# A list scheduler that counts a transfer's landing when it frees a buffer, with re-measured costs

## Chip, cores and metric

One core of a Trainium2 chip (trn2) runs the whole program. The time of a run is the device time in microseconds (us); the figure to predict is the median of the runs of the changed kernel.

## What is computed

Attention with talking heads, then a small mixture of matmuls with a softmax-like gate. Batch 4, 12 heads, 448 positions, head size 64; the second part has 1792 tokens, 768 in and 1024 hidden.

```python
scores = scale * np.matmul(q, k.transpose(0, 1, 3, 2))
scores = np.einsum('bhij,hg->bgij', scores, w_pre)
scores = scores - np.max(scores, axis=-1, keepdims=True)
attn = np.exp(scores)
attn = attn / (np.sum(attn, axis=-1, keepdims=True) + 1e-09)
attn = np.einsum('bhij,hg->bgij', attn, w_post)
x = np.matmul(attn, v)            # to (1792, 768)
h = x @ w_in
e = np.exp(h - np.max(h, axis=-1, keepdims=True))
solu = h * e / (np.sum(e, axis=-1, keepdims=True) + 1e-09)
ln = (solu - mean(solu)) / np.sqrt(var(solu) + 1e-06) * g_ln
out = ln @ w_out
```

## The kernel before

**Attention.** Every fp32 operand is split into a high and a low half in fp16. q, k and v of a batch are loaded in pieces, their largest magnitude is found on DVE (line 373; for v on ACT, line 371), they are scaled, and the halves are written: the high half on ACT (in batch 0) or POOL (line 217 or 219), the low half on DVE (line 222) or POOL (lines 406 and 407). The halves of q and k are turned by DMA transposes on SP's queue (`turn_in`, line 419; for k of batch 0 by PE), and a part of q is moved to other partitions (`move_hi`, line 464, in batch 0 on ACT's queue, else on SP's).

Scores are made in **blocks**, four to a batch, each of 120 or 88 query rows and all 12 heads. For each head `qk` (line 480) makes 448 scores per row in PSUM, `score_hi` (line 486, ACT) copies the high half to the block's tile `s`, and `score_lo` (line 491, DVE) writes the low half. There are two such tiles (ring `S`), so the first `score_hi` of a block needs the tile of the block two before to have been read out. A block is called (batch, number), as (1,0).

Then the work goes by **units** of 10 query rows, 45 to a batch. A `fetch` (line 509, SP) gathers the unit's rows for all 12 heads from `s` into one of three `sr` tiles (from SBUF to SBUF, 210 KB with all heads); `premix` (line 515, PE) mixes the heads; `rowmax` (line 520, DVE), `expo` (line 532, ACT), `guard` and `invert` (lines 546 and 549, DVE) and `weigh` (line 553, POOL) make the exponentials and the scaled mixing weights; `postmix` (line 561, PE) mixes again, and `post_out` (line 226, ACT) copies to `p_t`. When the units of a block are through, `av` (line 601, PE) multiplies by v, in two groups of heads, through one PSUM bank: the second group needs the first one read by `x_hi` (line 217, ACT) and `x_lo` (line 222, DVE). These write the batch's tiles `xsh` and `xsl`, of which there is one set (ring `X`), stored to DRAM by `x_store` (line 643, SP) in the next batch.

During the last batch w_in is loaded and split too, and the first matmuls of the second part (`h0`, line 764) are mixed in.

**What sets the order.** All of this is a list of about 2,850 tasks. Class `Plan` (lines 19 to 96) places them one by one: each has the engines that may run it with an assumed cost in us, the tasks it comes after, a due time, perhaps a ring (a number of buffers) with the tasks that free its buffer (`until`), and a latency `lat` that is added for whoever comes after it. Of the tasks that could start first, the one due first is taken. The instructions are then issued in that order, and each engine and queue of the chip runs its own in order; the plan's times are nowhere in the program. What the plan assumes, therefore, decides only which instruction stands before which.

A dependency counted `end + lat + 0.2`; a buffer's release counted the end of the freeing task plus 0.2, without its `lat`. `T0` and `STEP` (line 131) set the due times: unit u of batch b is due at T0 + STEP (45 b + u).

**The second part** is written out by hand behind the plan (lines 1145 to 1374) and is not touched.

Of the kernel before, what the change touches and what calls it, by code (L numbers as in the profile page):

```python
# [18 lines left out]
class Plan:  # L19
# [15 lines left out]
    def order(self):  # L35
        tasks, done, out = self.tasks, {}, []
# [9 lines left out]
        def ready(k, e):  # L46
            _, _, after, _, ring, _, _, _ = tasks[k]
            r = 0.0
            for a in after:
                end, eng, lat = done[a]  # L50
                r = max(r, end + lat + (0.06 if eng == e else self.WAIT))
            if ring and len(held[ring]) >= self.size[ring]:
                for a in held[ring][-self.size[ring]]:
                    if a not in done:
                        return None
                    r = max(r, done[a][0] + self.WAIT)
            return r

        last = {}
        while len(out) < len(tasks):  # L60
            best = None
            for e, t0 in free.items():
                able = []
                for k in avail:
                    on = tasks[k][1]
                    if e in on:
                        r = ready(k, e)
# [16 lines left out]
            run, on, _, _, ring, until, lat, _ = tasks[k]  # L84
# [15 lines left out]
def kernel(  # L100
# [26 lines left out]
    NU = (S + UN - 1) // UN  # L127
    NE, NWR = 4, 3
    WEIGH = {"pool": 0.36}
    AMV = {"act": 0.83}  # L130
    T0, STEP = 24, 2.17

    RING = 18
    SIZES = [[9, 12, 12, 12] if b % 2 == 0 else [12, 12, 12, 9] for b in range(B)]
# [638 lines left out]
    def add_tasks():  # L773
# [28 lines left out]
        for b in range(B):  # L802
# [3 lines left out]
            for n in "kq":  # L806
# [17 lines left out]
                for i in range(NP):  # L824
                    add(
                        ("am", n, b, i),
                        with_eng(absmax, n, b, i),
                        {"dve": 0.87},
                        after=[("ld", n, b, j) for j in range(pieces) if i * pieces < (j + 1) * NP and j * NP < (i + 1) * pieces]
                        + ["clear"],  # L830
                        due=at(b - 1, 15 + -4 * (n == "q")) + 3 * i if b else 4 * (n == "q") + i,
                    )
# [4 lines left out]
                for p in range(NPAIR):  # L837
                    due = at(b - 1, 24 + -4 * (n == "q") + 1 * p) if b else 12.0 + 6 * (n == "q") + 1.5 * p
                    add(
                        ("hi", n, b, p),  # L840
                        with_eng(pair_hi, n, b, p),
                        {"pool": 0.7} if b else {"act": 0.61},
                        after=ready + ([("hi", n, b, p - 1)] if p else before),
                        due=due,
                        ring=None if p else "hl",
                        until=[("tp", j) for j in range(NPAIR)] if z and n == "k" else [("t", n, b, j) for j, _ in turns[z]],
                    )
                    add(("lo", n, b, p), with_eng(pair_lo, n, b, p), {"dve": 0.66, "pool": 1.75} if b else {"dve": 0.66, "pool": 1.75}, after=[("hi", n, b, p)], due=due + 1)
                if z and n == "k":
                    for p in range(NPAIR):  # L850
                        due = 11 + 1.5 * p
# [10 lines left out]
                for p, m in turns[z] if not (z and n == "k") else ():  # L862
                    due = at(b - 1, 28 + 2 * p) if b else 14 + 3 * (n == "q") + 1.5 * p
                    add(
                        ("t", n, b, p),
                        one(turn_in, n, b, p, m),
                        {"sp": 1.2 if m == 1 else 1.95},
                        after=[("lo", n, b, j) for j in range(p, p + m)]
                        + ([] if z else [("qk", b - 1, NQ - 1, h) for h in range(2 * p, 2 * (p + m), 2)]),
                        due=due,  # L870
                        lat=2.0,
                    )
                    if n == "q":
                        add(
                            ("q1", b, p),
                            one(move_hi, b, p, m),
                            {"act": 0.1 * m} if z else {"sp": 0.7 * m},
                            after=[("t", n, b, p)] + [("cl", g) for g in range(NPAIR // GP)],
                            due=due + 1.5,
                            lat=2.6 if z else 2.1,  # L880
                        )
            add(("es", b), one(exp_scales, b), {"dve": 0.15}, after=es, due=at(b - 1, 35) if b else T0 - -2)

# [60 lines left out]
            for u in range(NU):  # L944
# [5 lines left out]
                add(  # L950
                    ("f",) + g,
                    one(fetch, *g),
                    {"sp": 0.9},
                    after=[("sl", b, blk, h) for h in range(H)],
                    behind=behind("f"),
                    due=d - 2 * STEP,
                    ring="sr",
                    until=[("m",) + g],
                    lat=2.0,
                )  # L960
                add(
                    ("m",) + g,
# [7 lines left out]
                add(  # L970
                    ("mx",) + g,
                    one(rowmax, *g),
                    {"dve": 0.6},
                    after=[("m",) + g, ("es", b)],
                    due=d + 0.5,
                    ring="e",
# [6 lines left out]
                    after=[("mx",) + g],  # L983
                    due=d + 1.2,
                )
                add(("gd",) + g, with_eng(guard, *g), {"dve": 0.08}, after=[("ex",) + g], due=d + 2)
                add(("iv",) + g, one(invert, *g), {"dve": 0.08}, after=[("gd",) + g], due=d + 2.2)
                add(
                    ("w",) + g,
                    with_eng(weigh, *g),  # L990
# [24 lines left out]
            for blk in range(NBLK[b]):  # L1015
# [3 lines left out]
                for g in range(NXG):  # L1019
# [12 lines left out]
                    add(  # L1032
                        ("xh", b, blk, g),
                        one(x_hi, b, blk, g),
                        {"act": 0.18 + 0.0007 * XG * n},
                        after=[("av", b, blk, g)] + ready,
                        due=due,
                        ring="X" if blk == g == 0 else None,
# [2 lines left out]
                    add(  # L1041
                        ("xl", b, blk, g),
                        one(x_lo, b, blk, g),
                        {"dve": 0.06 + 0.00105 * XG * n},
                        after=[("xh", b, blk, g)],
                        due=due + 0.5,
                    )
# [357 lines left out]
```

## Time and profile before

| | |
|---|---|
| median of 3 runs | 756.25 us (754.36 to 756.98) |
| the profiled execution's own time | 750.21 us |
| its span, first to last instruction | 748.2 us |
| mean granted TensorE clock | 0.974 of full |
| busy: DVE, ACT, POOL | 498.4, 447.8, 276.4 us |
| HBM read, written | 33.24 MB, 9.63 MB |

The profile shows one execution. "Busy" is time in which an engine ran instructions, "idle before" the time it stood still ahead of one, with the event that ended it. PE is TensorE, DVE VectorE, ACT ScalarE, POOL GpSimd, SP SyncE, which here only issues transfers ("SPq"). "Issue" as a releaser means that nothing in the profile explains the wait.

### The profile page before, as it was taken

Reading aid. Unit: us, or ns where it says so; the run is one execution under the profiler, and the core shown is the slowest. Engines: PE = TensorE matmul, PEld = TensorE weight load, DVE = VectorE, ACT = ScalarE, POOL = GpSimd, SP = SyncE. Lnnn points to the kernel's source line nnn. Section 1 sums busy time; section 2 is a strip of 40 time slices with the busy share of each in tenths; the row PEclk is TensorE's granted clock in tenths of the full one; section 3 lists DMA queues with packets and bytes.
Section 4 is the critical chain, followed back from the end, with each engine's and each line's share of the span. In section 5 each row is a group of like instructions: output and inputs, shape, how many; then the busy total and the mean of one; then the engine's idle time right before and its main releaser. Section 6 shows DMA issues by size and latency. Waiting matters only on the chain.

```text
span 748.2 us, 14777 instructions
## 1 busy us (share of the span) xinstructions
PE 669.7 (90%) x5206; PEld 483.5 (65%) x5206; DVE 498.4 (67%) x1484; ACT 447.8 (60%) x955; POOL 276.4 (37%) x381
## 2 busy tenths in 40 slices
PE   2589998999999889899899998899999857999998
PEld 1447777887877768777788777775444423566664
DVE  5569995677995658896578999875988764310000
ACT  1278786786776967777787887763555544331111
POOL 4605761133761114682112336440666642230000
PEclk9879999999999999999999999999999979999999
DMA  8546477245658426758425744517455422243112
GB/s 221 95 95 189 144 202 201 93 126 179 209 148 223 109 67 184 237 139 224 131 107 172 256 167 167 172 39 223 122 135 130 84 47 50 50 99 80 56 43 63
DMA packets 121473, 102.47 MB, mean 137 GB/s; under 512 B 75524, under 2 KB 112056, under 8 KB 121400
## 3 DMA queue, kind: packets, MB, share of 16 engines
q1 hardware_dynamic: 115128, 87.07, 41.8%
q0 software_dynamic: 4384, 12.40, 6.2%
q10 hardware_dynamic: 1888, 2.07, 1.1%
q8 instruction: 41, 0.67, 0.4%
q14 instruction: 32, 0.26, 0.1%
HBM read 33.24 MB, written 9.63 MB: 57 GB/s over the span
## 4 chain that ended last, share of the span: by engine, by line
PE 48%; DVE 22%; DMA 13%; POOL 6%; ACT 5%; issue 4%; SPq 1%; ACTq 0%; POOLq 0%; DVEq 0%
PE y L1314 14%; PE po L561 11%; PE pm L515 8%; DMA sr<-s 7%; PE ps L480 6%; PE px L601 6%; PE ps_h L764 4%; DVE s L491 4%; DVE e L520 3%; DMA raw_q<-in_q_dram 2%; DVE cv_wo L699 2%; POOL wo L702 2%; ACT e L532 1%; DVE cv_wo L694 1%; DVE u L1257 1%
## 5 line engine op out<-in xcount | busy, mean ns | idle before, releaser
L561 PEld LDWEIGHTS po<-wr,e 120*112 120x112 f32 x1440 | 174.8, 179 | 25.7 <-POOL wr L553 12.0
L561 PE MATMUL po<-wr,e 120*112 120x120 f32 x1440 | 181.9, 270 | 5.7 <-POOL wr L553 4.6
L553 POOL TENSOR_SCALAR wr<-wq,sm 120x120 f32<-120x120 f32 x180 | 77.7, 433 | 276.4 <-DVE sm L549 169.5
L532 ACT ACTIVATE e<-pm,nb,c_exp 120x448 f32<-120x448 f32 x180 | 131.0, 728 | 31.6 <-DVE e L520 17.7
L491 DVE SCALAR_TENSOR_TENSOR s<-ps,s 120x448 f16<-120x448 f32 (+1 forms) x192 | 116.7, 617 | 37.5 <-ACT s L486 31.4
L486 ACT ACTIVATE s<-ps 120x448 f16<-120x448 f32 (+1 forms) x192 | 104.0, 547 | 49.0 <-PE ps L480 28.5
L520 DVE TENSOR_SCALAR_CACHE_REDUCE e<-pm,c_nexp 120x448 f32<-120x448 f32 x180 | 121.2, 676 | 18.1 <-PE pm L515 13.5
L480 PE MATMUL ps<-k,q 128*120 128x448 f16 (+1 forms) x384 | 108.5, 367 | 18.5 <-DVE s L491 9.4
L226 ACT COPY p_t<-po 112x480 f32<-112x480 f32 x180 | 103.9, 577 | 24.3 <-PE po L561 23.5
L515 PE MATMUL pm<-sr,wp_hi 120*120 120x448 f16 x360 | 100.7, 362 | 15.2 <-DMA sr<-s 8.3
L764 PE MATMUL ps_h<-wi,xf 128*128 128x512 f16 x396 | 87.0, 379 | 2.5 <-DVE u L1257 2.5
L601 PE MATMUL px<-p_t,raw_v 112*64 112x120 f32 (+1 forms) x1536 | 80.7, 261 | 3.5 <-DVE xsl L222 2.7
L601 PEld LDWEIGHTS px<-p_t,raw_v 112*64 112x64 f32 x1536 | 73.9, 137 | 12.6 <-issue 7.3
L1314 PE MATMUL y<-wo_h,lth 128*128 128x384 f16 (+2 forms) x224 | 72.7, 331 | 9.7 <-ACT wo_h L217 9.7
L1314 PE MATMUL y<-wo_l,lth 128*128 128x384 f16 (+2 forms) x224 | 72.5, 330 | 2.5 <-DVE wo_l L222 2.0
L480 PEld LDWEIGHTS <-q 128*120 128x120 f16 (+1 forms) x384 | 48.5, 134 | 38.7 <-issue 21.6
L1314 PEld LDWEIGHTS <-lth 128*128 128x128 f16 x448 | 44.3, 99 | 43.7 <-issue 15.3
L1314 PE MATMUL y<-wo_h,ltl 128*128 128x384 f16 (+2 forms) x224 | 72.4, 330 | 0.0
L764 PEld LDWEIGHTS <-xf 128*128 128x128 f16 x396 | 38.6, 98 | 48.1 <-issue 3.0
L515 PE MATMUL pm<-sr,wp_lo 120*120 120x448 f16 x180 | 64.3, 357 | 0.0
L515 PEld LDWEIGHTS <-wp_hi 120*120 120x120 f16 x360 | 43.8, 135 | 31.4 <-DMA sr<-s 14.2
L1322 ACT ACTIVATE o<-y,c_out 128x384 f32<-128x384 f32 (+2 forms) x28 | 16.1, 578 | 72.4 <-PE y L1314 72.4
(168 smaller groups left out, 829.9 us busy)
## 6 DMA issues: line engine op xcount, KB each, us to landing
sr<-s SPq DMA_DIRECT2D x180, 210.0 KB
cv_wi<-in_moe_w_in_dram SPq DMA_DIRECT2D x24, 256.0 KB
cv_wo<-in_moe_w_out_dram SPq DMA_DIRECT2D x8, 768.0 KB
raw_k<-in_k_dram POOLq DMA_DIRECT2D x18, 224.0 KB, 4.6
raw_q<-in_q_dram POOLq DMA_DIRECT2D x18, 224.0 KB, 4.5
raw_v<-in_v_dram POOLq DMA_DIRECT2D x18, 224.0 KB, 3.6
q<-q SPq DMA_DIRECT2D x18, 112.0 KB
xh<-xsh SPq DMA_DIRECT2D x9, 224.0 KB
```

Source lines behind the costliest of these rows:

```text
L226: nc.scalar.copy(out=out, in_=in_)
L480: nc.tensor.matmul(y, x[:, e, i0 : i0 + n], k1[b, g][:, e], start=(a == 0), stop=(a == 1))
L486: nc.scalar.activation(out=s_t[b, c][0 : y.shape[0], h, 0], in_=y, func=AF.Copy, scale=2.0**-E_S)
L491: nc.vector.scalar_tensor_tensor(out=t[:, h, 1], in0=y, scalar=2.0**-E_S, in1=t[:, h, 0], op0=ALU.mult, op1=ALU.subtract)
L515: nc.tensor.matmul(ps[:, 0:S], w[0:UK], x[:, z], start=(a == 0), stop=(a == 2))
L520: nc.vector.tensor_scalar(out=e, in0=pmx[b, u][:, 0:S], scalar1=c_nexp[0:UK, b : b + 1], scalar2=None, op0=ALU.mult, op1=ALU.min, accum_ou ...
L532: nc.scalar.activation(out=ee[b, u], in_=pmx.pop((b, u))[:, 0:S], func=AF.Exp, bias=nbs.pop((b, u)), scale=c_exp[0:UK, b : b + 1], accum_o ...
L553: ENG[eng].tensor_scalar(out=w, in0=wq[0:UK, 0 : H * UN], scalar1=sums.pop((b, u)), scalar2=1.0, op0=ALU.mult, op1=ALU.mult)
L561: nc.tensor.matmul(ps[:, c * 120 : (c + 1) * 120], e[:, c * CP : (c + 1) * CP], w, start=True, stop=True)
L601: nc.tensor.matmul(xps[b, blk, g][e * 64 : e * 64 + 64, i, 0:n], raws["v", b][:, h, c * D : (c + 1) * D], block_view(b, blk, c * H + h), s ...
L764: nc.tensor.matmul(ps[:, n], xx[:, kc, o : o + 128], ww[:, kc, n * 512 : (n + 1) * 512], start=(kc == 0 and a == 0), stop=(kc == KDM - 1 a ...
L1314: nc.tensor.matmul(y, xx[:, kc], ww[:, kc, cut], start=(kc == 0 and a == 0), stop=(kc == KFF - 1 and a == 2),)
```

## The change

The release of a ring's buffer now counts the freeing task's `lat`. Beside it, assumed costs and latencies are replaced by others: fetches, transposes and moves on SP, the splits of q and k, the maxima, and the high and low halves of x. STEP grows from 2.17 to 2.25, so later units are due later. The number of tasks stays 2,846.

```diff
-                    r = max(r, done[a][0] + self.WAIT)
+                    r = max(r, done[a][0] + done[a][2] + self.WAIT)
...
-    AMV = {"act": 0.83}
-    T0, STEP = 24, 2.17
+    AMV = {"act": 0.95}
+    T0, STEP = 24, 2.25
...
-                        {"dve": 0.87},
+                        {"dve": 0.93},
...
-                        {"pool": 0.7} if b else {"act": 0.61},
+                        {"pool": 0.8} if b else {"act": 0.61},
...
-                    add(("lo", n, b, p), with_eng(pair_lo, n, b, p), {"dve": 0.66, "pool": 1.75} if b else {"dve": 0.66, "pool": 1.75}, after=[("hi", n, b, p)], due=due + 1)
+                    add(("lo", n, b, p), with_eng(pair_lo, n, b, p), {"dve": 0.85, "pool": 2.2} if b else {"dve": 0.66, "pool": 1.75}, after=[("hi", n, b, p)], due=due + 1)
...
                     one(fetch, *g),
-                    {"sp": 0.9},
+                    {"sp": 0.85},
...
                     until=[("m",) + g],
-                    lat=2.0,
+                    lat=2.7,
...
                         one(x_lo, b, blk, g),
-                        {"dve": 0.06 + 0.00105 * XG * n},
+                        {"dve": 0.76},
```

Left out are like lines: the transposes (1.2 or 1.95 to 1.75 on SP from batch 1 on, latency 2.0 to 2.4), the moves (0.7 to 0.6 per pair on SP, latency 2.1 to 2.6), `rowmax` (0.6 to 0.63), `guard` (0.08 to 0.1), `invert` (0.08 to 0.12) and `x_hi` (0.18 + 0.0007 x 3 n to 0.5, n rows of the block).

What it moves shows in the built programs' orders. Names there carry their numbers: `s_1_0` is the score tile of block (1,0), `ps_1_0_0` its head 0 in PSUM, `e_0_29` the exponentials of batch 0, unit 29, `po` a postmix, `ja_v` the maxima of v.

**ACT at block (1,0).** Its tile is freed by the fetches of block (0,2), whose last unit is 32. Before:

```order
L532 ACTIVATE e_0_27_1476,sm_0_27_1488<-pm_0_27_1409,nb_0_27_1475,c_exp_74 120x448
L226 COPY p_t_128<-po_0_25_1481 112x48x10
L486 ACTIVATE s_1_0_1504<-ps_1_0_0_1490 120x448
L532 ACTIVATE e_0_28_1494,sm_0_28_1508<-pm_0_28_1456,nb_0_28_1493,c_exp_74 120x448
L226 COPY p_t_128<-po_0_26_1499 112x48x10
L532 ACTIVATE e_0_29_1524,sm_0_29_1534<-pm_0_29_1471,nb_0_29_1523,c_exp_74 120x448
L226 COPY p_t_128<-po_0_27_1517 112x48x10
L532 ACTIVATE e_0_30_1537,sm_0_30_1555<-pm_0_30_1512,nb_0_30_1536,c_exp_74 120x448
L532 ACTIVATE e_0_31_1547,sm_0_31_1567<-pm_0_31_1529,nb_0_31_1546,c_exp_74 120x448
L226 COPY p_t_128<-po_0_28_1550 112x48x10
L486 ACTIVATE s_1_0_1504<-ps_1_0_1_1541 120x448
L532 ACTIVATE e_0_32_1575,sm_0_32_1592<-pm_0_32_1561,nb_0_32_1574,c_exp_74 120x448
```

Now:

```order
L226 COPY p_t_128<-po_0_26_1492 112x48x10
L532 ACTIVATE e_0_29_1506,sm_0_29_1529<-pm_0_29_1466,nb_0_29_1505,c_exp_74 120x448
L486 ACTIVATE s_1_0_1540<-ps_1_0_0_1483 120x448
L486 ACTIVATE s_1_0_1540<-ps_1_0_1_1502 120x448
L226 COPY p_t_128<-po_0_27_1535 112x48x10
L371 ACTIVATE ja_v13_1565,am_v1_149<-raw_v1_951 112x768
L532 ACTIVATE e_0_30_1561,sm_0_30_1578<-pm_0_30_1515,nb_0_30_1560,c_exp_74 120x448
L226 COPY p_t_128<-po_0_28_1555 112x48x10
L532 ACTIVATE e_0_31_1581,sm_0_31_1596<-pm_0_31_1524,nb_0_31_1580,c_exp_74 120x448
L226 COPY p_t_128<-po_0_29_1573 112x48x10
L532 ACTIVATE e_0_32_1590,sm_0_32_1610<-pm_0_32_1546,nb_0_32_1589,c_exp_74 120x448
L486 ACTIVATE s_1_0_1540<-ps_1_0_2_1568 120x448
```

The first copy of `s_1_0` stood ahead of the exponentials of units 28 to 32, five of the old block; now it stands behind 29 and ahead of three.

**ACT at the start.** `q1` is the moved part of q, one DMA per pair of heads (pairs 0 and 1 into `q1_0`, and so on). Before:

```order
L217 ACTIVATE hl_q0_300<-raw_q0_192,p2_q0_139 112x8x64 x6
L464 DMA q1_0_125<-q_0_0_345 64x896 x2
L464 DMA q1_1_126<-q_0_1_370 64x896 x2
L486 ACTIVATE s_0_0_408<-ps_0_0_0_400 88x448
L486 ACTIVATE s_0_0_408<-ps_0_0_1_405 88x448
L464 DMA q1_2_127<-q_0_2_389 64x896
L486 ACTIVATE s_0_0_408<-ps_0_0_2_412 88x448
L486 ACTIVATE s_0_0_408<-ps_0_0_3_418 88x448
```

Now:

```order
L217 ACTIVATE hl_q0_277<-raw_q0_192,p2_q0_139 112x8x64 x3
L464 DMA q1_0_125<-q_0_0_318 64x896 x2
L486 ACTIVATE s_0_0_398<-ps_0_0_0_392 88x448
L464 DMA q1_1_126<-q_0_1_362 64x896
L486 ACTIVATE s_0_0_398<-ps_0_0_1_400 88x448
L486 ACTIVATE s_0_0_398<-ps_0_0_2_412 88x448
L464 DMA q1_1_126<-q_0_1_362 64x896
L486 ACTIVATE s_0_0_398<-ps_0_0_3_418 88x448
L486 ACTIVATE s_0_0_398<-ps_0_0_4_429 88x448
L464 DMA q1_2_127<-q_0_2_395 64x896
```

The first copy of the scores stood behind the moves of pairs 0 to 3; now it stands behind those of pairs 0 and 1, and the other moves stand between the copies. (A row with x2 holds two pairs.)

**DVE at the x buffer of batch 2.** `xsl2` is that batch's tile of low halves, whose predecessor is drained by the stores of batch 1. Before:

```order
L520 TENSOR_SCALAR e_2_13_4039,nb_2_13_4038<-pm_2_13_4006,c_nexp_75 120x448
L222 SCALAR_TENSOR_TENSOR hl_k3_3979<-raw_k3_3574,p2_k3_163,hl_k3_3979 112x8x64
L546 TENSOR_SCALAR sm_2_12_4036<-sm_2_12_4036 120x1
L491 SCALAR_TENSOR_TENSOR s_2_2_3827<-ps_2_2_8_4025,s_2_2_3827 120x448
L549 RECIPROCAL sm_2_12_4036<-sm_2_12_4036 120x1
L222 SCALAR_TENSOR_TENSOR xsl2_4052<-px_2_0_0_3951,x_sc_77,xsh2_4051 128x80 x3
L222 SCALAR_TENSOR_TENSOR xsl2_4052<-px_2_0_0_3951,x_sc_77,xsh2_4051 128x3x8
```

Now:

```order
L373 TENSOR_REDUCE am_q3_164<-raw_q3_3782 112x1
L491 SCALAR_TENSOR_TENSOR s_2_2_3827<-ps_2_2_9_4032,s_2_2_3827 120x448
L210 TENSOR_REDUCE amx_q3_165<-am_q3_164 128x1
L546 TENSOR_SCALAR sm_2_13_4055<-sm_2_13_4055 120x1
L491 SCALAR_TENSOR_TENSOR s_2_2_3827<-ps_2_2_10_4049,s_2_2_3827 120x448
L549 RECIPROCAL sm_2_13_4055<-sm_2_13_4055 120x1
L520 TENSOR_SCALAR e_2_14_4084,nb_2_14_4083<-pm_2_14_4041,c_nexp_75 120x448
L199 TENSOR_REDUCE amx_q3_165<-spread_q3_4079 128x1
L491 SCALAR_TENSOR_TENSOR s_2_2_3827<-ps_2_2_11_4074,s_2_2_3827 120x448
L163 TENSOR_SCALAR p2_q3_166<-amx_q3_165 128x1
L222 SCALAR_TENSOR_TENSOR xsl2_4094<-px_2_0_0_3952,x_sc_77,xsh2_4093 128x80 x3
L222 SCALAR_TENSOR_TENSOR xsl2_4094<-px_2_0_0_3952,x_sc_77,xsh2_4093 128x3x8
```

The first write of `xsl2` stood behind head 8 of the block's low halves and the row maximum of unit 13; now behind head 11 and unit 14.

## Rows read from the trace of the kernel before

**Rows 1.** The page, part 1: PE's busy us, share of the span, instructions.
```profile
PE 669.7 (90%) x5206; PEld 483.5 (65%) x5206; DVE 498.4 (67%) x1484; ACT 447.8 (60%) x955; POOL 276.4 (37%) x381
```

**Rows 2.** Stretches: us, busy (instructions) per engine, PEclk, DMA share, GB/s.
```profile
50.59:511.60 461.01, 426.34 (x3909) 352.94 (x3910) 365.28 (x1174) 341.71 (x788) 180.60 (x298) 0.98 0.55 163
```

**Rows 3.** Waits of ACT; columns: us in total, times, longest.
```profile
ACT s L486 <- DMA sr<-s: 7.4, 3, 3.7
ACT s L486 <- issue: 7.0, 2, 3.8
```

**Rows 4.** Timeline of ACT, three first copies: start, duration, instruction, [idle before <- releaser].
```profile
271.25 0.54 ACT L486 ACTIVATE s<-ps 120x448 f16<-120x448 f32 x1 [3.75 <-issue]
...
327.65 0.54 ACT L486 ACTIVATE s<-ps 120x448 f16<-120x448 f32 x1 [2.22 <-DMA sr<-s]
...
416.30 0.54 ACT L486 ACTIVATE s<-ps 120x448 f16<-120x448 f32 x1
```

**Rows 5.** Timeline of SP, the fetches that free these buffers.
```profile
265.79 0.77 SPq L509 DMA_DIRECT2D sr<-s  x1
...
323.02 0.77 SPq L509 DMA_DIRECT2D sr<-s  x1
```

**Rows 6.** Timeline of PE behind these copies.
```profile
125.84 0.90 PE L515 MATMUL pm<-sr,wp_hi 120*120 120x448 f16 x2 [2.61 <-ACT e L532]
...
154.99 0.54 PE L515 MATMUL pm<-sr,wp_hi 120*120 120x448 f16 x2 [0.57 <-ACT e L532]
...
245.27 0.90 PE L480 MATMUL ps<-k,q 128*88 128x448 f16 x2 [2.74 <-DVE s L491]
...
272.50 0.91 PE L480 MATMUL ps<-k,q 128*120 128x448 f16 x2 [2.99 <-DVE s L491]
...
328.90 0.54 PE L480 MATMUL ps<-k,q 128*120 128x448 f16 x2 [0.72 <-DVE s L491]
...
359.98 0.54 PE L515 MATMUL pm<-sr,wp_hi 120*120 120x448 f16 x2 [2.04 <-ACT e L532]
```

**Rows 7.** Stretches, three with these waits, one without; columns as before.
```profile
124.00:129.00 5.00, 3.16 (x13) 2.48 (x13) 3.25 (x13) 4.28 (x11) 0.73 (x2) 0.66 0.51 136
270.00:277.00 7.00, 4.50 (x22) 3.73 (x22) 3.49 (x11) 4.05 (x9) 0.36 (x1) 0.76 0.10 30
280.00:290.00 10.00, 10.00 (x108) 8.69 (x107) 7.92 (x24) 8.50 (x21) 5.23 (x10) 1.00 0.60 170
358.00:366.00 8.00, 5.75 (x31) 4.82 (x32) 4.90 (x18) 7.09 (x18) 1.09 (x3) 0.79 0.36 118
```

**Rows 8.** Timelines of SP, DVE and PE, the x buffer at batch 2.
```profile
312.21 0.55 SPq L643 DMA_DIRECT2D xl<-xsl  x1
...
316.30 0.87 DVE L222 SCALAR_TENSOR_TENSOR xsl<-px,x_sc,xsh 128x80 f16<-128x80 f32 x4 [1.81 <-DMA xl<-xsl]
...
317.43 0.79 PE L601 MATMUL px<-p_t,raw_v 112*64 112x88 f32 x15 [2.41 <-DVE xsl L222]
```

**Rows 9.** Page, part 5: DVE's low half; after the bar: busy us, mean ns.
```profile
L491 DVE SCALAR_TENSOR_TENSOR s<-ps,s 120x448 f16<-120x448 f32 (+1 forms) x192 | 116.7, 617 | 37.5 <-ACT s L486 31.4
```

**Rows 10.** Timelines of ACT, PE and SP, the start.
```profile
31.50 0.47 ACTq L464 DMA_DIRECT2D q<-q  x1
...
37.60 0.60 PE L480 MATMUL ps<-k,q 128*88 128x448 f16 x1 [5.75 <-DMA q<-q]
...
38.28 0.54 ACT L486 ACTIVATE s<-ps 88x448 f16<-88x448 f32 x1 [14.39 <-PE ps L480]
...
46.71 1.01 SPq L509 DMA_DIRECT2D sr<-s  x1
```

**Rows 11.** Chain that ended last, 495 to 530 us: start, us, what.
```profile
511.64 11.78 PE ps_h L764 x54
```

**Rows 12.** Waits of PE; columns as above.
```profile
PE pm L515 <- DMA sr<-s: 8.3, 13, 1.6
```

**Rows 13.** Waits of SP's queue; columns as above.
```profile
SPq L419 <- DVE sm L549: 7.3, 3, 3.0
```

More of the change, by code (lines that the diff above doesn't have):

```diff
@@ L866, in add_tasks @@
                         one(turn_in, n, b, p, m),
-                        {"sp": 1.2 if m == 1 else 1.95},
+                        {"sp": 1.75 if b else 1.95},
                         after=[("lo", n, b, j) for j in range(p, p + m)]
@@ L870, in add_tasks @@
                         due=due,
-                        lat=2.0,
+                        lat=2.4,
                     )
@@ L876, in add_tasks @@
                             one(move_hi, b, p, m),
-                            {"act": 0.1 * m} if z else {"sp": 0.7 * m},
+                            {"act": 0.1 * m} if z else {"sp": 0.6 * m},
                             after=[("t", n, b, p)] + [("cl", g) for g in range(NPAIR // GP)],
                             due=due + 1.5,
-                            lat=2.6 if z else 2.1,
+                            lat=2.6,
                         )
@@ L958, in add_tasks @@
                     until=[("m",) + g],
-                    lat=2.0,
+                    lat=2.7,
                 )
@@ L972, in add_tasks @@
                     one(rowmax, *g),
-                    {"dve": 0.6},
+                    {"dve": 0.63},
                     after=[("m",) + g, ("es", b)],
@@ L985, in add_tasks @@
                 )
-                add(("gd",) + g, with_eng(guard, *g), {"dve": 0.08}, after=[("ex",) + g], due=d + 2)
-                add(("iv",) + g, one(invert, *g), {"dve": 0.08}, after=[("gd",) + g], due=d + 2.2)
+                add(("gd",) + g, with_eng(guard, *g), {"dve": 0.1}, after=[("ex",) + g], due=d + 2)
+                add(("iv",) + g, one(invert, *g), {"dve": 0.12}, after=[("gd",) + g], due=d + 2.2)
                 add(
@@ L1034, in add_tasks @@
                         one(x_hi, b, blk, g),
-                        {"act": 0.18 + 0.0007 * XG * n},
+                        {"act": 0.5},
                         after=[("av", b, blk, g)] + ready,
```

## The prediction

> **What bounds the kernel now.** I read the page first. TensorE (PE) works 90% of the span [rows 1], far ahead of every other engine. The table by stretches then tells where the missing tenth lies. From the first premix at 50.59 us to the last product with V at 511.6 us PE is busy 426 of 461 us, at a mean clock of 0.98 [rows 2]. So this stage, attention, is bound by PE, and what can be had there is some 35 us of idle time and the time at half speed. The stage behind it runs the same code in both kernels and can only start earlier or later.
>
> Next I asked who waits. On ACT the copies that store the high half of the scores (line 486) wait for "DMA sr<-s", or for nothing that the profile can name ("issue"), 14.4 us in five waits, up to 3.8 us each [rows 3]. The timeline shows where: each is the first copy of a block of scores [rows 4]. A block is written into one of two S buffers, and the buffer comes free when the last fetch of the block two before has landed. In the block with first copy at 271.25 us that fetch went out at 265.79, so 5.5 us passed; in the one at 327.65 it went out at 323.02, 4.6 us [rows 4, 5]. ACT was free 3.75 and 2.22 us earlier and stood still, and with it every exponential behind that copy.
>
> PE pays for it [rows 6]: 2.61, 0.57, 2.74, 2.99, 0.72 and 2.04 us idle right behind six of these copies, 11.7 us. After four of the waits its matmuls take twice their time: a pair of premixes 0.90 us, where 0.54 is usual [rows 6]. The granted clock falls to means of 0.66 over 5 us, 0.76 over 7 and 0.79 over 8, and is 1.00 in a stretch without such a wait [rows 7]; that is 1.7 us of work lost each time (0.34 x 5, 0.24 x 7, 0.21 x 8), the drop to the lower of the two levels, 1.2 GHz. The fourth, at 245 us, has the same doubled rows and is counted alike: 6.8 us. All in all the S buffers cost 11.7 + 6.8 = 18.5 us.
>
> A second buffer with this fault holds the attention output x. At batch 2 the last of its stores goes out at 312.21 us; DVE waits for its landing until 316.30, and PE's next product waits 2.41 us for DVE [rows 8].
>
> **The change part by part.** *Landing counted in the release.* No instruction is added or dropped; the scheduler places those that reuse a buffer filled or drained by a transfer later. I count how many exponentials of the block being read out still stand behind the first copy of the new block on ACT. For the 14 blocks from the third on it was 2, 2, 5, 5, 2, 2, 5, 3, 1, 3, 4, 2, 2, 4; it is now 3, 2, 3, 2, 2, 2, 3, 2, 1, 2, 1, 2, 2, 2. The trace of before says what these numbers are worth: all six PE waits above lie at a 3, 4 or 5 (one more 4 cost PE nothing); at a 1 or 2 (the row at 416.30) the copy follows without a wait, or with one that PE does not feel [rows 4, 6]. Four of the six are thus turned to a 1 or a 2. Three 3s stand in the new order. Blocks (1,0) and (2,0) have the copy directly behind an exponential, as the block at 271.25 had it, so I price each by that nearest row: 2.99 + 1.7 = 4.7 us. Block (0,2) has two other copies in between, as the one at 327.65, so 0.72. What is left is 10.1 us, the gain 18.5 - 10.1 = **8.4 us**. Ends: all three like the dear row, gain 4.4; all like the cheap one, gain 16.3.
>
> The Trainium skill would price the landing lower: "DMA: Bandwidth & Descriptors", section "Anatomy of one DMA", gives about 2.0 us fixed plus bytes over 436 GB/s, fitted on transfers that GpSimd issues, so as an estimate 2.5 us for the fetch's 210 KB. Here the trace disagrees, with 4.6 and 5.5 us; by that rule a copy directly behind an exponential, which ACT reaches 1.7 us after the fetch's issue (271.25 - 3.75 - 265.79), would wait 0.8 us, PE would not feel it, and the gain would be the whole 18.5 us.
>
> *The x buffer.* DVE's step for batch 2 now stands behind three more low-half steps of the scores, 0.62 us each [rows 9], and one more row maximum, so at least 1.85 us later; the wait was 1.81 us [rows 8]. On PE eleven groups of matmuls stood between the product before and the one that waited, and now sixteen. I take the 2.41 us as gone; ends 0 and 2.4. No gain is claimed at batches 1 and 3, where nothing waited.
>
> *The start.* ACT's first copy (38.28 us) stood behind four moves of q; in the new order it stands behind the first two, the second of which was issued at 31.50 and took 0.47 us [rows 10]. At best everything up to the first fetch (46.71 us) comes 38.28 - 31.97 = 6.3 us earlier. But now the later moves stand behind copies that need earlier moves. A move took from 31.50 to 37.60 until PE could use it, 6.1 us; three in a row from 31.50 end at 49.8, and with 2 us for the last copies the fetch would go 5 us late. Between a gain of 6.3 and a loss of 5 I take a gain of 1: the last pair's own move ends the chain in either order.
>
> *The end.* Five instead of nine tasks of the first MoE product stand behind the last product with V. At 11.78 us for 54 matmuls [rows 11], eight matmuls are 1.7 us. They only help where they fill PE's waits before it, so 1 us; ends 0 and 1.7, and a loss of 1.2 if the split of w_in (one DVE step) is late for the earlier place.
>
> *The new DVE, ACT and SP costs, STEP and the due times.* They only reorder. One low half goes from POOL to DVE, one high half of w_in from POOL to ACT, about 1 us each, hidden by the idle fifth of DVE and quarter of ACT in this stage [rows 2] and costing that much where they are late. Premixes that wait for a fetch cost PE 8.3 us [rows 12]; the units with less than 3.6 us of PE work between the premix that frees the fetch buffer and the one that uses it go from 12 to 10, too little to claim more than 0; ends 1.4 either way (two twelfths).
>
> **Sum:** 8.4 + 2.4 + 1 + 1 = 12.8 us off the profiled execution's 750.2, so 737.4. That execution ran 6 us under the median of the runs, 756.25, so for the median I forecast **743.5 us**. With all the better ends (16.3 + 2.4 + 6.3 + 1.7) it is 729.5, with all the worse ones (4.4 and 0 gained, the start late by 5, the end by 1.2, the fetches by 1.4) 759.5.
>
> **Rivals.** *The wait only changes its place.* ACT goes on, but PE then stops at what DVE delivers, and nothing of the 8.4 us stays: with the x buffer alone 753.9. For it: a list schedule deals all waits anew. Against it: in stretches without an S wait PE is busy all the time at full clock (10.00 of 10 us) with DVE at 7.9 [rows 7], so DVE has room. Chance 0.11.
>
> *Slower: transposes hold the fetches.* SP issues in order. The key transposes of batch 1 stood behind the fetches of units 24, 27 and 29 and now stand behind 29, 31 and 32, while their low halves are made beside units 19 to 26 instead of 12 to 17. A transpose that has to wait for its input holds every fetch behind it, and PE stops at the premix. Price: up to 3.0 us per hold [rows 13] and 1.7 for the clock, 4.7. Three holds (14.1) undo the 12.8 us; with four it is 756.25 - 12.8 + 18.8 = 762. For it: the margin between the last low half of the first one and its turn on SP shrinks from some eight units to one. Against it: in batches 2 and 3 the first key transpose stays within one unit of its place, and the scores of a block are finished six units before its first use in both orders. Chance 0.13.
>
> *No copy waits any more.* If the three remaining copies stand far enough back for their fetches to have landed, the S term is the whole 18.5 us: 18.5 + 4.4 = 22.9 us, 733.4. Against it: two of them stand as close behind an exponential as the block at 271.25 did, which waited 3.75 us [rows 4]; for it: the block at 154.99 lost 0.57 us only, with the copy placed worse [rows 6]. Chance 0.06. The figure of the Trainium skill's page above would lead here.
>
> **How the numbers follow.** My forecast has 0.70. A measurement of this kernel can tell about 0.3%, 2.3 us, from no change. Faster by more: most of the forecast (0.68) and the third rival, with a little of the first, 0.76. Within: the rest of the first rival and the forecast's worst end, 0.11. Slower: the held fetches, 0.13. The range goes from 731, near the better ends, to 756, beyond the first rival's 753.9; it leaves out the slower rival and the outermost of both ends.
>
> **What would show it.** Right: on ACT no first copy with more than 1.5 us of idle before it, but at (1,0), (2,0) and perhaps (0,2); half-speed stretches in attention two instead of four; DVE's wait for the x stores gone; attention's PE idle time under 28 us; from the end of the last product with V to the end some 235 us, as before. Wrong: as many half-speed stretches as before, behind other waits; SP's transposes waiting longer in sum; a first fetch later than 47 us.

## The result, and the profile after

| | before | changed kernel |
|---|---|---|
| first comparison, 4 runs each, median | 755.31 us | 731.5 us (728.95 to 737.7) |
| the same kernel again, 6 runs (11 of before) | 751.93 us | 733.28 us (731.89 to 738.29) |
| profiled execution: time, span | 750.21, 748.2 us | 728.95, 727.2 us |

The ratio is 0.971 (95% interval 0.963 to 0.979) in the first comparison and 0.974 (0.971 to 0.978) in the second. The forecast was 743.5 over 756.25, or 0.983: the direction is right, the time lies just inside the good end of the range, and the gain is 1.5 to 1.7 times the forecast one.

Page, part 1, answering [rows 1], and the table by stretches from the first premix to the last product with V, answering [rows 2]:

```profile
PE 659.5 (91%) x5206; PEld 479.8 (66%) x5206; DVE 495.4 (68%) x1485; ACT 449.9 (62%) x956; POOL 273.2 (38%) x378
```

```profile
46.06:490.97 444.91, 420.20 (x3917) 352.37 (x3918) 362.04 (x1175) 343.46 (x789) 178.02 (x295) 0.99 0.57 168
```

The span lost 21.0 us in three pieces: the first premix comes 4.5 us earlier (46.06 for 50.59), attention takes 16.1 us less (444.9 for 461.0; PE idle 24.7 for 34.7, busy 420.2 for 426.3), and 0.4 us come from the stage behind.

First copies of blocks on ACT with their fetch on SP, answering [rows 4, 5] (columns: start, duration, instruction, idle before it and what ended it):

```profile
63.23 0.54 ACT L486 ACTIVATE s<-ps 120x448 f16<-120x448 f32 x1 [3.23 <-DMA sr<-s]
...
119.03 0.99 ACT L486 ACTIVATE s<-ps 120x448 f16<-120x448 f32 x2
...
237.03 0.97 ACT L486 ACTIVATE s<-ps 88x448 f16<-88x448 f32 x2 [2.82 <-DMA sr<-s]
...
261.29 0.98 ACT L486 ACTIVATE s<-ps 120x448 f16<-120x448 f32 x2 [1.64 <-issue]
```

```profile
56.45 0.77 SPq L509 DMA_DIRECT2D sr<-s  x1
```

These are blocks (0,2), (1,0), (2,0) and (2,1). Eleven of the 14 copies wait for nothing, (1,0) among them; these three wait.

PE at these places, answering [rows 6], and stretches, answering [rows 7]:

```profile
63.05 0.54 PE L515 MATMUL pm<-sr,wp_hi 120*120 120x448 f16 x2 [1.86 <-DMA sr<-s]
...
124.78 1.00 PE L515 MATMUL pm<-sr,wp_hi 120*120 120x448 f16 x2 [2.24 <-DMA sr<-s]
...
235.99 0.59 PE L515 MATMUL pm<-sr,wp_hi 120*120 120x448 f16 x2 [2.89 <-DMA sr<-s]
...
237.56 0.95 PE L515 MATMUL pm<-sr,wp_hi 120*120 120x448 f16 x2
...
262.55 0.54 PE L480 MATMUL ps<-k,q 128*120 128x448 f16 x2 [1.24 <-DVE s L491]
```

```profile
120.00:131.00 11.00, 8.76 (x57) 7.05 (x56) 7.02 (x26) 7.15 (x19) 1.24 (x5) 0.84 0.66 160
232.00:244.00 12.00, 8.84 (x49) 6.76 (x48) 6.40 (x23) 7.06 (x19) 1.46 (x4) 0.86 0.62 159
```

Behind the waits of 2.24 and 2.89 us the matmuls take twice their time, 1.00 and 0.95 us a pair where 0.54 is usual. Two stretches behind waits at the lower level of the clock are left where four were, and 0.16 x 11 and 0.14 x 12 give 1.8 and 1.7 us, the price that the prediction used.

Of these waits only the one of 1.24 us at 262.55 is what the prediction called an S wait, one in which PE waits for work that a first copy held up on ACT (the copy at 261.29). At 63.05 and 235.99 PE waits for the rows that the premix itself reads, those of units 8 of batch 0 and 34 of batch 1, which it needs whatever the copy does. At 235.99 they come with another fetch than the one that frees the buffer: ACT still waits until 237.03. So the S buffers cost PE 1.2 us instead of 18.5, and the other waits belong to the fetches. SP shows what stands ahead of two of these, and when the fetch was issued that frees the buffer of (2,1):

```profile
115.58 1.85 SPq L419 DMA_TRANSPOSE k<-hl_k  x1
117.48 2.42 SPq L419 DMA_TRANSPOSE q<-hl_q  x1
120.00 1.75 SPq L509 DMA_DIRECT2D sr<-s  x2
...
231.38 1.64 SPq L419 DMA_TRANSPOSE q<-hl_q  x1
233.13 1.79 SPq L509 DMA_DIRECT2D sr<-s  x2
...
255.87 0.77 SPq L509 DMA_DIRECT2D sr<-s  x1
```

Transposes stand right ahead of the fetches at 120.00 and 233.13. They keep SP for 4.3 and 1.6 us by their own length; a wait for their input, by which the second rival had them hold the fetches, does not show. Waits of PE in whole, answering [rows 12]:

```profile
PE pm L515 <- DMA sr<-s: 19.8, 14, 2.9
...
PE po L561 <- POOL wr L553: 2.6, 4, 0.9
...
PE ps L480 <- DVE s L491: 2.5, 3, 1.2
```

Waits for a fetch rose from 8.3 to 19.8 us. The wait for the x stores [rows 8] is in the list no more. The start, from the chain of waits:

```profile
23.21 1.47 POOL hl_q L407
...
24.70 3.88 DMA q<-hl_q
...
28.66 3.67 DMA q<-q
...
33.38 3.82 DMA q<-q
...
37.73 2.10 DMA q<-q
...
42.05 3.87 DMA sr<-s
```

POOL makes the low half of q's pair 1 at 23.21; in the chain of before this stood at 27.11. A move here takes 2.1 to 3.8 us until PE goes on, not the 6.1 of [rows 10]; with the new costs alone (experiment 1) one took 6.3 again.

### The profile page after: what moved, and what is told of

Its sections match the earlier page's. It is cut to its first block, busy times and chain, and to the rows that moved or that the text cites. A ratio compares the mean times of both kernels' runs of the same rounds, so it can differ in the third digit from the quotient of the medians.

```text
span 727.2 us, 14776 instructions
## 1 busy us (share of the span) xinstructions
PE 659.5 (91%) x5206; PEld 479.8 (66%) x5206; DVE 495.4 (68%) x1485; ACT 449.9 (62%) x956; POOL 273.2 (38%) x378
## 4 chain that ended last, share of the span: by engine, by line
PE 60%; DVE 14%; DMA 14%; POOL 6%; ACT 3%; issue 2%; ACTq 0%; SPq 0%; POOLq 0%; DVEq 0%
PE po L561 15%; PE y L1314 14%; PE pm L515 11%; DMA sr<-s 10%; PE px L601 8%; PE ps L480 8%; PE ps_h L764 3%; DVE cv_wo L699 2%; POOL wo L702 2%; DMA raw_q<-in_q_dram 2%; DVE u L1257 1%; DVE cv_wo L694 1%; DMA q<-q 1%; DVE e L520 1%; DVE wi L222 1%
## 5 line engine op out<-in xcount | busy, mean ns | idle before, releaser
L561 PE MATMUL po<-wr,e 120*112 120x120 f32 x1440 | 179.0, 268 | 2.8 <-POOL wr L553 2.6
L532 ACT ACTIVATE e<-pm,nb,c_exp 120x448 f32<-120x448 f32 x180 | 131.9, 734 | 18.5 <-DVE e L520 9.7
L515 PE MATMUL pm<-sr,wp_hi 120*120 120x448 f16 x360 | 101.1, 362 | 21.5 <-DMA sr<-s 19.8
L480 PE MATMUL ps<-k,q 128*120 128x448 f16 (+1 forms) x384 | 106.6, 359 | 7.6 <-DMA q<-q 4.8
L1322 ACT ACTIVATE o<-y,c_out 128x384 f32<-128x384 f32 (+2 forms) x28 | 16.1, 578 | 72.4 <-PE y L1314 72.4
```

The costliest lines, as they stand in the source:

```text
L480: nc.tensor.matmul(y, x[:, e, i0 : i0 + n], k1[b, g][:, e], start=(a == 0), stop=(a == 1))
L515: nc.tensor.matmul(ps[:, 0:S], w[0:UK], x[:, z], start=(a == 0), stop=(a == 2))
L532: nc.scalar.activation(out=ee[b, u], in_=pmx.pop((b, u))[:, 0:S], func=AF.Exp, bias=nbs.pop((b, u)), scale=c_exp[0:UK, b : b + 1], accum_o ...
L561: nc.tensor.matmul(ps[:, c * 120 : (c + 1) * 120], e[:, c * CP : (c + 1) * CP], w, start=True, stop=True)
```

## Experiments

The theory: the line on the release ends most of the S waits, and that is the bulk of the gain. Rivals: the measured costs do it; the waits only change places; or the new order is a lucky deal. Ratios are to the runs of before on the same chip.

**1. The line alone, the costs alone.** The line, in the kernel before:

```diff
-                    r = max(r, done[a][0] + self.WAIT)
+                    r = max(r, done[a][0] + done[a][2] + self.WAIT)
```

> The kernel before with one line of the change: the release of a buffer counts the landing of the last transfer out of it. Nothing in batch 0's start moves (four moves of q stay ahead of the first copy on ACT; GpSimd's low halves stay k5, q1, q4). The exponentials of the old block behind a first copy become 2,2,3,3,2,2,4,2,1,2,2,2,2,2 where they were 2,2,5,5,2,2,5,3,1,3,4,2,2,4. Theory (the S buffer's waits are the main term, and this line alone removes them): first copies wait under 3 us in all beside one at the start of batch 2, the attention stretch (first premix to the end of the last weighted sum) falls from 461 by 8 to 12 us, the start stays (first fetch issued at 46.7 us), total about 741 to 746. Rival (the measured costs do it; the line alone moves the waits to the next fetches): attention within 4 us of 461, total 750 or more.

And the change without this line:

> The change without that line: only the measured costs and transfer times. The first copies keep 3,3,3,3,2,3,5,3,1,4,3,3,3,2 exponentials behind them; batch 0 starts as in the changed kernel (two moves of q ahead of the first copy, GpSimd's low halves q1, q2, q4). Theory: the start gains what the changed kernel's gained (first premix 4 to 5 us earlier than 50.6), the waits of first copies stay near half of the 18 us, so attention falls by 3 to 8 us; total 741 to 748. Rival (the costs do it all): total 731 to 735 as in the changed kernel.

The line: 737.21 us, ratio 0.981 (0.978 to 0.985). The costs: 749.06 us, 0.998 (0.994 to 1.001). Stretches of attention, and the worst wait behind a first copy, in the line's trace and then in that of the costs:

```profile
50.68:497.35 446.67, 424.15 (x3913) 351.55 (x3914) 364.46 (x1175) 343.20 (x790) 173.62 (x294) 0.99 0.57 168
...
263.49 0.54 PE L480 MATMUL ps<-k,q 128*120 128x448 f16 x2 [1.96 <-DVE s L491]
```

```profile
47.79:510.00 462.21, 427.78 (x3925) 356.60 (x3926) 362.94 (x1175) 340.45 (x787) 176.48 (x297) 0.97 0.55 162
...
240.35 0.90 PE L480 MATMUL ps<-k,q 128*88 128x448 f16 x2 [4.51 <-DVE s L491]
```

The line takes 14.4 us out of attention, more than the 8 to 12 expected, and leaves the start alone; of the S waits that PE feels one of 1.96 us remains. The costs bring the start 2.8 us forward, not 4 to 5, and leave attention at 462, where 3 to 8 us less were expected: behind first copies PE waits 4.51, 2.35 and 2.37 us. PE's waits for a fetch, 8.3 us before, are 14.3 with the line alone and 21.2 with the costs alone.

**2. Which buffer.** The line for the ring S alone, and for all rings but S:

```diff
+                    r = max(r, done[a][0] + (done[a][2] if ring == "S" else 0) + self.WAIT)
...
+                    r = max(r, done[a][0] + (done[a][2] if ring != "S" else 0) + self.WAIT)
```

> The kernel before with the release line for the ring of the S buffers alone; every other buffer is released as before. The exponentials of the old block behind the first copies become 2,2,3,3,2,2,4,2,1,2,3,3,2,3. The release line for all buffers gave 14 us (737 against 752). Theory (the S buffer is what that line corrects): attention 444 to 452 us instead of 461, the waits of first copies under 8 us in all, total 738 to 744. Rival (the line works through the other buffers, the high and low halves that wait for the transposes and the x buffer): attention above 456 us, total above 748.

> The kernel before with the release line for all buffers but S. The first copies keep the most behind them: 2,2,5,5,2,2,5,3,1,3,2,2,3,4. Theory (S): the waits of first copies stay near 16 us, and of the 14 us of the line for all buffers at most the x buffer's 2 to 4 show: attention 456 to 461 us, total 747 to 752. Rival (the other buffers do it): attention 444 to 450 us, total 738 to 743. A re-dealt order that is good or bad by chance would show as a number outside both.

S alone: 736.63 us, 0.977 (0.973 to 0.980). The others: 749.97 us, 0.994 (0.992 to 0.997). With S alone:

```profile
49.67:498.73 449.06, 422.81 (x3909) 351.42 (x3910) 367.03 (x1174) 340.79 (x788) 178.01 (x298) 0.99 0.57 167
...
263.86 0.54 PE L480 MATMUL ps<-k,q 128*120 128x448 f16 x2 [1.95 <-DVE s L491]
...
306.33 1.45 PE L601 MATMUL px<-p_t,raw_v 112*64 112x88 f32 x28 [2.39 <-DVE xsl L222]
```

With the others alone:

```profile
48.57:513.22 464.65, 427.58 (x3913) 353.37 (x3914) 363.92 (x1175) 344.52 (x790) 173.00 (x294) 0.98 0.55 161
...
246.40 0.91 PE L480 MATMUL ps<-k,q 128*88 128x448 f16 x2 [3.06 <-DVE s L491]
...
273.81 0.91 PE L480 MATMUL ps<-k,q 128*120 128x448 f16 x2 [2.99 <-DVE s L491]
```

This tells the S ring from the others. With S counted one S wait of 1.95 us is left and the wait for x stays, 2.39 us; with the others counted the two dear S waits and their doubled rows stay and the wait for x goes, and attention is 3.6 us longer than before, outside the 456 to 461 that were expected.

**3. Only the copies held back.** The order of before, in which seven first copies on ACT stand behind the old block's last-but-one exponential; nothing else is priced anew. (`held_back` gives the tasks out in the order of before, with these waits added.)

```diff
-        for _, e, _, run in plan.order():
+        ends = [(b, u1 - 1) for b in range(B) for u1 in BLK0[b][1:]]
+        extra = {}
+        for j in (4, 5, 8, 9, 11, 12, 15):
+            b, u = ends[j - 2]
+            extra["sh", j // NQ, j % NQ, 0] = [("ex", b, u - 1)]
+        for _, e, _, run in held_back(plan, extra):
```

> The kernel before with its own order, in which only the first copy of seven blocks (those with three or more exponentials of the old block behind them) is held until the old block's last-but-one exponential has been given to ACT. Costs, start, moves of q, transposes stay. Theory (the stalls of those copies on ACT, with the half-speed stretches behind them, cost what the prediction added up): attention falls from 461 by 11 to 17 us, less up to 4 for copies that now stand in a row ahead of products; total 737 to 745. Rival (the wait only changes place: the next block's first premix or first fetch is late by as much): attention within 4 us of 461, total 750 to 758.

748.23 us, 0.996 (0.993 to 0.998), between the two forecasts: attention 458.0 us, 3.0 less, not 11 to 17.

```profile
49.07:507.10 458.03, 424.00 (x3909) 351.31 (x3910) 364.87 (x1174) 343.03 (x788) 180.66 (x298) 0.99 0.56 164
```

ACT, then PE, at block (2,0):

```profile
240.00 0.96 ACT L486 ACTIVATE s<-ps 88x448 f16<-88x448 f32 x2
241.81 1.07 ACT L486 ACTIVATE s<-ps 88x448 f16<-88x448 f32 x2 [0.85 <-PE ps L480]
243.66 0.54 ACT L486 ACTIVATE s<-ps 88x448 f16<-88x448 f32 x1 [0.77 <-PE ps L480]
```

```profile
241.24 1.07 PE L480 MATMUL ps<-k,q 128*88 128x448 f16 x4 [1.06 <-DVE s L491]
243.06 1.44 PE L480 MATMUL ps<-k,q 128*88 128x448 f16 x4 [0.75 <-DVE s L491]
```

None of the seven copies stalls ACT any more, but PE's order is that of before: products of the new block now come in a row with their copies and wait for them. The waits "ps <- DVE s" went from 9 with 9.4 us to 14 with 10.4. So the first rival is right for a copy moved by itself. With the line the scheduler deals the products anew as well; that it gains for this reason is argued and not shown.

**4. The start.** The order of before with the moves of q of pairs 2 to 5 held behind copies; then the same, with POOL making the low halves of q's pairs 1, 2 and 4 and DVE that of k's pair 5.

```diff
+        extra = {("q1", 0, p): [("sh", 0, 0, 2 * p - 4)] for p in range(2, NPAIR)}
...
+        made = {("lo", "k", 0, 5): "dve", ("lo", "q", 0, 2): "pool"}
```

> The kernel before with its own order, in which only the moves of q of pairs 2 to 5 of batch 0 are held behind four of the first block's copies on ACT. Theory of the prediction (the last pair's own move ends the chain in either order): the first fetch is at most 1 us earlier than 46.7. Rival (the moves held the first copy): the first copy starts some 5 us or more earlier and the first fetch 3 to 5 us earlier, as in the changed kernel. Third (the low half that GpSimd makes earlier in the changed kernel decides it): nothing changes here, and the start gains only where that order is changed too. Attention after the start is unchanged within 3 us in all three.

> The kernel before with its own order and two edits in batch 0 alone: the moves of q of pairs 2 to 5 held behind copies, as in the experiment on the moves, and GpSimd making the low halves of q1, q2, q4 (k's pair 5 goes to DVE in place of q's pair 2), as in the changed kernel. The moves alone brought the first fetch from 46.7 to 45.6. Theory (the low half of pair 1, 2.6 us earlier on GpSimd, carries the transposes of q, and with the moves out of the way the last pair's product): the first fetch is issued at 41.5 to 43.5. Rival (the start gains from something else in the changed order, such as which engine makes the high halves): 44.5 to 46. The attention behind it is unchanged within 4 us, so total 747 to 751 by the theory.

The moves alone: 752.77 us, 1.001 (0.998 to 1.003). The first copy starts at 31.40, 6.9 us earlier, and the first fetch only 1.1 us earlier:

```profile
35.05 3.65 DMA q<-q
...
41.31 2.09 DMA q<-q
...
45.62 3.86 DMA sr<-s
```

Attention behind it took 465.2 us, 4.1 more than before, where at most 3 were expected.

With the low halves the first fetch goes out at 43.68, 3.0 us earlier than before and 0.2 past what was expected. The total is 756.06 us, 1.003 (0.999 to 1.006), not 747 to 751: attention took 5 us more, with two half-speed stretches that before did not have, so a gain at the start can be lost in the same run. Of the changed kernel's 4.7 us at the first fetch 1.1 came with the moves, 1.9 more with the low halves, and 1.6 were not taken apart.

**5. A deal for no reason, and a longer landing.** The changed kernel with

```diff
-    T0, STEP = 24, 2.25
+    T0, STEP = 24, 2.24
```

> The changed kernel with its pacing step 2.24 in place of 2.25, a number that prices nothing: the whole order is dealt anew, with 3,1,3,2,2,2,3,2,1,2,3,3,2,1 exponentials behind the first copies. It measures how far an order that counts landings moves for no reason. Theory (what the change brings is its rule): 729 to 740. Rival (a good part of the change's 21 us is one lucky deal): 740 to 748, as where the fetch was priced at 3.6 us, with new waits in other places and half speed behind them.

and, in another kernel, with a fetch priced at `lat=3.6` instead of 2.7:

> The changed kernel with one number more: a fetch is priced at 3.6 us of landing where the change says 2.7 (the traces show 3.4 to 6.8 from the issue of the last fetch to the copy behind it). First copies keep 2,2,2,2,2,2,3,2,2,1,2,2,2,1 exponentials behind them where the changed kernel keeps 3,2,3,2,2,2,3,2,1,2,1,2,2,2, and the key transposes of batch 1 stand behind fetches 23, 26, 29 again where they stood behind 29, 31, 32. Theory (what is left of the S waits, some 7.7 us, and the premix behind two transposes in a row, 2.2 us, are worth their price): 3 to 8 us under the changed kernel, 724 to 729. Rival (no more to be had: earlier fetches' waits or the copies' lateness take it back): 730 to 736.

> The changed kernel as it is, once more, so that the two beside it are compared with its own runs of the same chip. Every theory expects what it gave before: 729 to 738, a ratio near 0.971. In its profile: the two PE waits for a fetch near 125 and 236 us (2.2 and 2.9 us) and half speed behind both, since they come from the order and not from chance.

The step: 739.02 us, 0.982 (0.979 to 0.985), at the far end of what the theory allowed. The longer landing: 743.09 us, 0.986 (0.982 to 0.989), slower than the theory and the rival had it. Both are slower than the changed kernel itself, 733.28. In the longer landing's trace PE's longest wait behind a copy is 0.7 us, but new waits stand elsewhere, one of 3.30 us for a fetch (114.45); here PE, then POOL:

```profile
433.36 3.07 PE L561 MATMUL po<-wr,e 120*112 120x120 f32 x16 [2.85 <-POOL wr L553]
```

```profile
429.10 2.90 POOL L702 TENSOR_TENSOR wi<-cv_wi 128x1024 f32<-128x1024 f32 x1 [2.00 <-DVE sm L549]
431.98 1.67 POOL L553 TENSOR_SCALAR wr<-wq,sm 120x120 f32<-120x120 f32 x2
```

A step of w_in's conversion, priced at 2.35 us and here 2.90, got ahead of the weights that PE was to use, and PE fell to half speed behind it (granted clock 0.79 from 431 to 439).

So how a deal falls is worth several us. Five orders count the landing for S: 0.977, 0.981, 0.974, 0.982 and 0.986, mean 0.980. Three do not: 1, 0.998 and 0.994, mean 0.997. The difference, 0.017, is 13 us of 752. The worst of the five beats the best of the three. The rule is thus worth some 13 us, and the changed kernel is the best of five deals; with so few, that is an estimate.

**6. Transposes out of the way.** The changed kernel's order, with the last transposes of q of batches 1 and 2 held behind fetch 35; then their moves too (the last line, in the second kernel alone):

```diff
+        extra = {}
+        for b, u in (1, 37), (2, 38):
+            extra["t", "q", b, 4] = [("f", b - 1, 35)]
+            extra["q1", b, 4] = [("f", b - 1, u)]
```

> The changed kernel with its own order, in which only two transposes of q on SP (of the last pair group of batches 1 and 2) are held behind fetch 35 of the running batch, so that no transpose stands right ahead of the fetches at 120.00 and 233.13. Theory of the second rival of the prediction (a transpose ahead of a fetch costs its hold, and at two units of lead PE then waits and falls to half speed): the waits of 2.2 and 2.9 us fall under 1.3, the half-speed stretches behind them go, attention 3 to 6 us shorter, total 3 to 6 under the changed kernel's own runs. Rival (the fetches land late for other reasons, or the products of those pairs of heads now wait for the held transpose): within 2 us of it.

> The kernel of the experiment on the two transposes, with one step more: the moves of q that wait for those transposes to land (batches 1 and 2, last pair group) stand behind fetches 37 and 38 of the running batch. In that experiment the move of batch 2 stood right behind its transpose, waited 5.6 us on SP for it to land, and PE waited 5.08 us for the fetch behind it (243.19). Theory (what holds a fetch is the wait of the move for the transpose, and a place with two or three fetches between covers it): that wait and its half-speed stretch go, no wait near 125 or 236 to 243 is over 1.5 us, total 3 to 8 us under the changed kernel's 733, 725 to 730. Rival (the products of those heads now wait for the late moves, or the waits only move on): a wait of PE for a move of q over 1.5 us shows near 130 or 245, total 731 to 735.

The transposes alone: 732.42 us, 0.973 (0.970 to 0.975), no different from the changed kernel, where 3 to 6 us less were expected. SP, then PE, at batch 2:

```profile
232.55 1.51 SPq L419 DMA_TRANSPOSE q<-hl_q  x1
238.14 1.17 SPq L464 DMA_DIRECT2D q<-q  x2
239.42 0.86 SPq L509 DMA_DIRECT2D sr<-s  x1
```

```profile
243.19 1.00 PE L515 MATMUL pm<-sr,wp_hi 120*120 120x448 f16 x2 [5.08 <-DMA sr<-s]
```

The move stood right behind its transpose, went out 5.6 us after it, and the fetch behind it came too late. With the moves two and three fetches behind the transposes: **726.55 us, 0.963 (0.960 to 0.968)**, better than both kernels and inside the 725 to 730 expected.

```profile
46.35:486.89 440.54, 418.32 (x3917) 349.92 (x3918) 361.65 (x1175) 344.08 (x789) 178.18 (x295) 1.00 0.57 170
120.00:131.00 11.00, 10.26 (x84) 8.04 (x84) 8.76 (x34) 10.33 (x26) 1.84 (x5) 1.00 0.78 195
...
232.09 0.59 PE L515 MATMUL pm<-sr,wp_hi 120*120 120x448 f16 x2 [1.99 <-DMA sr<-s]
```

The wait near 125 is gone; the one at 232 is 1.99 us, over the 1.5 that was expected, yet no half speed follows it. Behind the start no stretch of attention is at half speed any more.

## Why the prediction was right and wrong

| step of the prediction | forecast | profiled execution | verdict |
|---|---|---|---|
| S waits | 8.4 | 18.5 - 1.2 = 17.3 | right mechanism; what is left was priced far too high |
| x buffer | 2.4 | 2.4 | right; stays with S alone, goes with the others |
| start | 1 | 4.5 | too small |
| end | 1 | 0.4 | too large |
| all else | 0 | -3.6 | wrong: the fetches are late |
| sum | 12.8 | 21.0 | |

That the time lies in the range is in part luck: the S waits and the start gave 12.4 us more than forecast, all else and the end took 4.2 of them back.

*S waits.* The theory held: the line for the S ring alone does the work. The step that failed is the price of the three 3s, 10.1 us. None of them cost PE anything that shows: the copy of (1,0) waits for nothing, those of (0,2) and (2,0) hold ACT for 3.23 and 2.82 us, but PE waits at that time for fetches of its own. What is left, 1.2 us, lies at (2,1), a 2. The count of exponentials behind a copy is a weak measure: in the kernel with the line alone a 4 cost ACT 0.58 us, the two 3s 0.27 and nothing, but a 2, again at (2,1), 2.41. What decides is whether ACT gets there before the landing, and at (2,1) the landing seems to be late, though the profile names no event that ends this wait. In every profiled execution in which this copy waits it starts 5.4 to 5.5 us behind the issue of the last fetch of the block two before (265.79 to 271.25 before, 255.87 to 261.29 now), at (2,0) 2.9 (234.10 to 237.03). That last fetch, of a block of 88 rows, gathers ten neighbouring rows, where those of a full unit stand 8 or 12 apart (lines 498 to 509); whether this makes it slow no run tells. The dear row by which the prediction priced two of the 3s was this block's, the one at 271.25. In the kernel with the line alone the S waits cost 2.0 us, so the term is 16.5 there, the forecast's better end.

The Trainium skill's page "DMA: Bandwidth & Descriptors", section "Anatomy of one DMA", gave an estimate of 2.5 us for this fetch. The fastest fetches here come near it: the premix at 235.99 goes on 2.9 us after its fetch was issued at 233.13. It is no price for all of them: the copy at 63.23 waited 6.8 us from the fetch's issue at 56.45. The third rival's condition did not come about, since three copies still wait on ACT; its price for the S waits, 18.5 us, nearly did.

*The start.* "The last pair's own move ends the chain in either order" is right for the moves, 1.1 us in the experiment. What the step left out is POOL's order: pair 1's low half before k's pair 5. It read ACT's moves and not the engine ahead of them.

*The end.* Eight matmuls fewer stand behind the last product with V, 1.7 us by the prediction's price, but PE waits there for DVE 3.6 us instead of 2.5 (line 764), and the stage is only 0.4 us shorter.

*All else.* "They only reorder", with ends of 1.4 us for the fetch waits, failed. PE's waits for a fetch rose by 11.5 us, and the two half-speed stretches that are left, 3.5 us, stand behind two of them; the measure that the prediction used, units with little work between two premixes, pointed the other way (12 to 10). Against it PE's other waits in attention fell by 8.1 us (weights from POOL 4.6 to 2.6, w_in's step 2.0 to none, and others). Eight matmuls more stand in attention, 1.7 us, and some 5 us of PE's busy time went without a wait that names them. PE's weight loads for the postmix waited 12.0 us for POOL before and 5.2 after, which may be a part of it; no run takes it apart.

*Rivals.* That the wait only changes its place is true where a copy alone is moved (experiment 3). That transposes hold the fetches happened at two places, not at three or four: 2.24 and 2.89 us with 1.8 and 1.7 of clock, each a little under the 4.7 priced. Moving these transposes and their moves gave some 7 us (experiment 6).

*What would show it.* Half-speed stretches two for four, idle 24.7 under 28, x gone, 236.2 us behind: right. No copy over 1.5 us but at three blocks: (2,1) has 1.64, (1,0) none.

*The size.* A mean deal with the line gives some 13 us. That this is what was forecast is chance, since the forecast's 12.8 also holds the x buffer, the start and the end. The deal that was measured is better than the mean one by some 5. The prediction treated the order's remainder as 1.4 us either way; the runs put it at about 5.

## What to carry to other kernels

When a planner frees a buffer at the end of the issue and not of the landing, the fault shows as first users that stand still on an in-order engine: count the landing there first, before any other cost. Moving the late user alone handed most of the wait to the next engine here, so look at those who feed and follow it too. A cost that is measured better does not make the order better by itself: a list schedule's deals spread by some 9 us here, so compare several deals of a rule with several without it, then mend the last waits by hand in the trace.

## What was not expected of the hardware

The same program with the same order was profiled at 728.95 and at 738.29 us. In the second, attention has four stretches at half speed behind waits and not two:

```profile
47.52:500.28 452.76, 426.71 (x3917) 356.78 (x3918) 361.46 (x1175) 343.55 (x789) 178.27 (x295) 0.97 0.56 165
...
442.22 0.91 PE L515 MATMUL pm<-sr,wp_hi 120*120 120x448 f16 x2 [3.13 <-DMA sr<-s]
```

Equal fetches of 210 KB land at different times, and the clock multiplies it: the fetch behind this wait was issued at 434.62, 7.6 us earlier, and in the first execution the same one at 428.62, 5.9 us before its premix (434.51, a wait of 1.42). From the issue of a block's last fetch to the copy that waited for its landing it took between 2.8 us (before, 441.96 to 444.74) and 7.1 (second kernel of experiment 6, 56.68 to 63.75). And the length of a wait alone does not tell whether the clock falls. Two waits of 1.06 and 0.75 us close together were followed by its lower level (experiment 3: four products in 1.07, then in 1.44 us; granted clock 0.79 from 240 to 248), as was one of 1.70 us (the line alone, 435.25; granted clock 0.66 from 435 to 440). One of 1.99 us (experiment 6) and one of 2.03 (the changed kernel, 402.39; granted clock 1.00 from 402 to 408) were not.
